# A third recursive product in a two-level Strassen-Winograd kernel, with differences written over the raw weights

## Chip, cores and metric

The kernel runs on one core of a Trainium2 chip. The metric is the device time of one execution in microseconds. TensorE (PE in the profile) multiplies, ScalarE (ACT) and VectorE (DVE) move results out of PSUM, the accumulators' memory of 8 banks, and form sums; SyncE (SP) issues the DMAs. Each engine takes its instructions in order; semaphores order the engines among each other.

## What is computed

```python
def _A_ref(x, wqkv, wo):
    q, k, v = ...x @ wqkv...           # 32 heads of 32
    phi = lambda t: jnp.where(t > 0, t + 1, jnp.exp(t)) + 1e-6
    pq, pk = phi(q), phi(k)
    kv = jnp.einsum("bhsd,bhse->bhde", pk, v)
    z = jnp.einsum("bhsd->bhd", pk)
    num = jnp.einsum("bhqd,bhde->bhqe", pq, kv)
    den = jnp.einsum("bhqd,bhd->bhq", pq, z)[..., None] + 1e-6
    return (num / den)... @ wo

def _B_ref(x, w_gate, w_up, w_down):
    return (_silu(x @ w_gate) * (x @ w_up)) @ w_down

xn = _layernorm(x)                     # x: 2048 x 1024
return x + _A_ref(xn, ...) * _silu(_B_ref(xn, ...))
```

The gate and up weights are 1024 x 3584, the down weights 3584 x 1024; inputs and output are bf16.

## The kernel before

**Stages.** Layer norm and the k and v projections with the sum over positions come first (some 120 us). Then a loop over weight blocks of 512 columns, `for k, n in order` (line 1431), for each of two halves of the positions, p = 0 and 1: gate blocks ("g", n), up blocks ("u", n), n = 0 to 6, and two blocks ("q", n) of the query projection. After ("u", 3) four attention-output pairs (`s_pair`, line 1221, one for each 512 positions) multiply the normalised queries by a matrix that holds kv and wo together. The gated products go to memory, and four groups (`Group`) read them back for the down projection.

**A pair.** Nearly every product of matrices is a 2 x 2 block product done with seven block products in place of eight. The seven products are called m = 1 to 7. Products 1, 2 and 4 use raw blocks of the stationary operand (here the weights), 5, 6, 7 and 3 use sums or differences of them, which `sums` (line 958) forms on VectorE. A `Set` (line 487) holds seven products for 128 stationary columns; its `step(m)` issues four matmuls 128x128 times 128x512 and the additions behind them. Two sets, 0 and 1, make a `Pair`: the step "7_1" is product 7 of set 1.

**A joint.** Products 1 and 5 of both sets of a pair are themselves one 2 x 2 block product, and `Joint` (line 551) does it with seven inner products of two matmuls of 256 columns each. Its four steps a to d need results of one another: step a issues inner products 1 and 5 and lets ScalarE copy both out of the bank, steps b and c each let VectorE add two results, step d is the last. "j1b" is step b of the joint for product 1. `inner_stat` (line 995) makes the sums of the stationary operand for the joints, `inner_move` (line 1022) those of the moving one (the activations), once for each half. After a joint for product 1 `put1` copies the result to a second bank; after one for product 5 `put5` copies it to SBUF.

**Order.** Within a pair the order is written out by hand: `LINK` (line 607) interleaves the end of one pair with the joints of the next, so that other matmuls stand between the steps of a joint ("n" marks steps of the next pair):

```python
LINK = "7_0 nj1a 3_0 7_1 nj1b nj5a 3_1 nj1c nj5b 4_0 nj1d nj5c 4_1 n2_0 nj5d n6_0 n2_1 n6_1".split()
```

On this a planner works when the program is built (`Plan.schedule`, line 91): it knows a cost of each instruction and fixes the order on each engine for good. PE may take an instruction early only within `WINDOW` = 6 groups of matmuls; VectorE and ScalarE take what is ready, most urgent first; a DMA is issued when what it overwrites is done with and its due time is near. `emit` (line 186) turns dependencies into semaphore waits.

**Weights.** `wload` (line 968) loads a block (1 MB) into one of two raw slots (`raw_ring`, 8 KB per partition) and writes four sums into one of two slots of `cmb_ring` (8 KB), and the joints' sums into `in_ring` (four slots of 2 KB, four sums each). Dependencies are tracked by region: a raw slot counts as one.

**Around the loop.** `m_build` (line 946) makes the combined matrix in 16 pieces that stand at steps of the first pairs (`BUILD`, line 1407). `recip` (line 1095) computes the denominators at ("g", 2), `normalise_part` (line 1125) multiplies the queries by them from ("u", 2) to ("g", 3). `phi_evac` (line 743) is the query's activation; with `split` ScalarE does a second pass over the tile in place of VectorE.

Of the kernel before, what the change touches and what calls it, by code (L numbers as in the profile page):

```python
# [239 lines left out]
def build_kernel(nc, A_x, A_wqkv, A_wo, B_w_gate, B_w_up, B_w_down, out, WINDOW=6, NWARM=14, NPE=4, LEAD=12.0):  # L240
# [12 lines left out]
    with ExitStack() as es:  # L253
# [178 lines left out]
        d_ring = Ring(TM, 4 * KB, 2 * KB, 2)  # L432
# [5 lines left out]
        x_ring = Ring(W, 36 * KB, 2 * KB, 4)  # L438
        xn_ring = Ring(W, 0, 2 * KB, 2)
        xs_ring = Ring(W, 44 * KB, 4 * KB, 2)  # L440
# [46 lines left out]
        class Set:  # L487
# [4 lines left out]
            def __init__(self, ops, evac, dring):  # L492
                self.ops, self.evac, self.dring, self.direct = ops, evac, dring, None
# [19 lines left out]

            def put5(self, e):
                self.s5 = s5_ring.take()
                act([bank_r[e]], [self.s5.r], self.s5.ap(F32), ps[e][:, :], ACT.Identity)
                bfree(e)

            def step(self, m):
# [11 lines left out]
                elif m == 6:  # L531
                    self.grp(6, self.b, False)
                    self.c = balloc()
                    tt([bank_r[self.b], self.s5.r], [bank_r[self.c]], ps[self.c][:, :], ps[self.b][:, :],
                       self.s5.ap(F32), ALU.add)
                elif m == 7:
                    self.grp(7, self.b, False)
                    if self.direct is not None:
                        self.direct(1, 1, self.b, self.s5)
                        return  # L540
                    d = self.dring.take()
                    tt([bank_r[self.b], self.s5.r], [d.r], d.ap(F32), ps[self.b][:, :], self.s5.ap(F32), ALU.add)
# [46 lines left out]
        class Pair:  # L589
# [3 lines left out]
            def __init__(self, s0, s1, joint, at):  # L593
                self.sets, self.joint, self.at = (s0, s1), joint, at

            def do(self, w):
                if w[0] == "j":
                    self.joint[w[1]].step("abcd".index(w[2]))
                else:
# [7 lines left out]
        LINK = "7_0 nj1a 3_0 7_1 nj1b nj5a 3_1 nj1c nj5b 4_0 nj1d nj5c 4_1 n2_0 nj5d n6_0 n2_1 n6_1".split()  # L607
        last_pair = [None]

        def feed(pair):  # L610

            prev = last_pair[0]
            if pair is None or not pair.joint:
                if prev is not None:
                    for w in TAIL:
                        prev.do(w)
# [3 lines left out]
            else:  # L620
                for w in LINK:
                    if w[0] == "n":
                        pair.do(w[1:])
                    elif prev is not None:
# [197 lines left out]
        def kv_set(u, w, stat):  # L822
# [16 lines left out]
            st = Set(ops, evac, d_ring)  # L839
# [118 lines left out]
        def sums(A, o, rd, wr):  # L958

            tt(rd, [wr[0]], o[0], A[0, 1], A[1, 1], ALU.add, True)  # L960
            tt(rd + [wr[0]], [wr[1]], o[1], o[0], A[0, 0], ALU.subtract, True)
            tt(rd, [wr[2]], o[2], A[0, 0], A[0, 1], ALU.subtract, True)
            tt(rd + [wr[1]], [wr[3]], o[3], A[1, 0], o[1], ALU.subtract, True)
# [4 lines left out]
        def wload(src, joint):  # L968
# [6 lines left out]
            cv = c.ap(FP16).rearrange("p (m w kt n) -> p m w kt n", m=4, w=2, n=128)  # L975
            cr = [c.sub(q * 2 * KB, 2 * KB).r for q in range(4)]
            sums({(k, i): v[:, :, 4 * k:4 * k + 4, i * 128:i * 128 + 128] for k in range(2) for i in range(2)},
                 [cv[:, q] for q in range(4)], [s.r], cr)

            def whole(m):  # L980
                if m in RAW_OF:
                    k, i = RAW_OF[m]
                    return v[:, :, 4 * k:4 * k + 4, i * 128:i * 128 + 128], s.r
                return cv[:, SUM_OF[m]], cr[SUM_OF[m]]

            def block(m):
                bl, r = whole(m)
                return (lambda k0, n, i: bl[:, i, k0:k0 + n, :]), r

            def stat(w, m):  # L990
                bl, r = whole(m)
                return [bl[:, w, q, :] for q in range(4)], r
            return stat, inner_stat(block, joint, 4, in_ring.take)

        def inner_stat(block, joint, kt, take):

            inner = {}
            for m in joint:
                bl, r = block(m)
                t = take()  # L1000
                n = kt // 2 * 256
                tv = t.ap(FP16, 0, 4 * n).rearrange("p (m kt n) -> p m kt n", m=4, n=128)
                tr = [t.sub(q * n, n).r for q in range(4)]
                A = {(k, i): bl(k * (kt // 2), kt // 2, i) for k in range(2) for i in range(2)}
                sums(A, [tv[:, q] for q in range(4)], [r], tr)
                inner[m] = (A, r, tv, tr)

            def jstat(m, k):
                A, r, tv, tr = inner[m]
                if k in RAW_OF:  # L1010
                    return [A[RAW_OF[k]][:, q, :] for q in range(kt // 2)], r
                return [tv[:, SUM_OF[k], q, :] for q in range(kt // 2)], tr[SUM_OF[k]]
            return jstat

        def xset(stat, w, xv, evac, dring):
# [4 lines left out]
            return Set(ops, evac, dring)  # L1020

        def inner_move(v, kt, at, raw=False, ms=(1, 5)):
# [17 lines left out]
        def in_places(arena, base, n):  # L1040
            return tuple(tuple((arena, base + (3 * m + q) * n) for q in range(3)) for m in range(2))
# [3 lines left out]
        def joint_of(jstat, xin, n, s0, s1):  # L1045
            def ops(m):
                def f(k):
# [4 lines left out]
            return {"1": Joint(ops(1), lambda w, b: (s0, s1)[w].put1(b)),  # L1052
                    "5": Joint(ops(5), lambda w, b: (s0, s1)[w].put5(b))}
# [17 lines left out]
        def q_load(s):  # L1071
            return wload(wqkv_v[:, :, s * 512:(s + 1) * 512], (1, 5))
# [10 lines left out]
        def q_pair(p, s, stats, at):  # L1083
            stat, jstat = stats

            def evac(w):
                def f(i, j, ap, r, bank):
                    g = 2 * (2 * s + w) + i
                    o, orr = pq_tile(p, g, j)
                    phi_evac(ap, r, o, orr, "ps" if bank is not None else "sb", i == 0)  # L1090
                return f
            s0, s1 = (xset(stat, w, XV[p], evac(w), d_ring) for w in range(2))
# [50 lines left out]
        def gu_load(k, n):  # L1143
            return wload((wg_v if k == "g" else wu_v)[:, :, n * 512:(n + 1) * 512], (1, 5))
# [13 lines left out]
        def gu_pair(p, kind, n, stats, at):  # L1158
# [38 lines left out]
            s0, s1 = (xset(stat, w, XV[p], (ev_g if kind == "g" else ev_u)(w), d_ring) for w in range(2))  # L1197
# [5 lines left out]
        def blocks(get, kt):  # L1203

            def block(m):
                ap, r = get(m)
                return (lambda k0, n, i: ap[:, k0:k0 + n, 128 * i:128 * i + 128]), r

            def stat(w, m):
                ap, r = get(m)  # L1210
                return [ap[:, q, 128 * w:128 * w + 128] for q in range(kt)], r
            return block, stat

        so_ring = Places([(TM, o * KB) for o in (8, 9, 12, 13)] + [(H, o * KB) for o in range(32, 40)], 1 * KB)
# [6 lines left out]
        def s_pair(g):  # L1221
            p, j0 = g // 2, g % 2
            A = {}
            for k in range(2):
                o = pq_off(p, k, j0)
                for i in range(2):
                    A[k, i] = (H.at(o, 4 * KB, FP16).rearrange("p (q t) -> p q t", t=512)[:, :, 256 * i:256 * i + 256],
                               H.reg(o, 4 * KB))
            c = ss_ring.take()
            cv = c.ap(FP16).rearrange("p (m q t) -> p m q t", m=4, t=256)  # L1230
            cr = [c.sub(q * 2 * KB, 2 * KB).r for q in range(4)]
            sums({q: a for q, (a, _) in A.items()}, [cv[:, q] for q in range(4)], [A[0, 0][1], A[1, 0][1]], cr)

            def get(m):
                return A[RAW_OF[m]] if m in RAW_OF else (cv[:, SUM_OF[m]], cr[SUM_OF[m]])
# [10 lines left out]
            s0, s1 = (xset(stat, w, MV, evac(w), d_ring) for w in range(2))  # L1246
            return Pair(s0, s1, joint_of(inner_stat(block, (1, 5), 4, in_ring.take), MIN, 2, s0, s1), {})
# [37 lines left out]
        DAT = (tuple((W, q * 3584) for q in range(3)), ((W, 28 * KB), (W, 28 * KB + 3584), (W, 43 * KB)))  # L1285
# [13 lines left out]
        hslots = Slots([(X, 0), (X, 7 * KB), (X, 14 * KB), (X, 21 * KB), (W, 20 * KB), (W, 36 * KB),  # L1299
                        (H, 7 * KB), (H, 14 * KB), (H, 21 * KB)], 7 * KB)  # L1300
        g_ring = Places([(W, o * KB) for o in (47, 48, 49, 50)], 1 * KB)
        sl_ring = Places([(W, o * KB) for o in (51, 27, 35, 19)], 1 * KB)
# [5 lines left out]
        class Group:  # L1308
# [50 lines left out]
            def dset(self, w):  # L1359
# [23 lines left out]
                return Set(ops, evac, d_ring)  # L1383
# [5 lines left out]
        XIN[1] = inner_move(XV[1], 4, in_places(W, 6 * KB, KB))  # L1389
# [4 lines left out]
        def fetch():  # L1394
            if lq:
                k, n = lq.popleft()
                return q_load(n) if k == "q" else gu_load(k, n)
# [5 lines left out]
        def build_m():  # L1403
            if mb:
                m_build(*mb.popleft())

        BUILD = {"2_0": [build_m], "6_0": [build_m], "2_1": [build_m] * 2, "6_1": [build_m] * 2}
        mb = deque((g, c) for c in range(2) for g in range(NG))
        AT = {("g", 0, 0): {"5_1": [kv_done], "3_0": [kvt]},
              ("g", 0, 1): BUILD, ("u", 0, 0): BUILD, ("u", 0, 1): BUILD,  # L1410
              ("g", 2, 0): {"6_1": [partial(recip, 0)]},
              ("g", 2, 1): {"6_1": [partial(recip, 1)]}}
        norm = [partial(normalise_part, p, j, half) for p in range(2) for j in range(2) for half in range(2)]
        for a, key in enumerate((("u", 2, 0), ("u", 2, 1), ("g", 3, 0), ("g", 3, 1))):
# [169 lines left out]
```

## Time and profile before

| | us |
|---|---|
| median of three runs (lowest, highest) | 717.33 (717.17, 718.4) |
| the profiled execution | 716.87 |
| its span, first to last instruction | 715.1 |
| TensorE busy | 705.0 |
| VectorE busy | 528.0 |
| ScalarE busy | 407.4 |

The profile is of one execution. A row of instructions has its start, its length, the engine, the source line (most lines are helpers': 229 issues matmuls, 359 ScalarE activations, 369 VectorE tensor-tensor operations, 372 DMAs), the operation, the tensors it writes and reads, its shape and how many alike were merged. X and P hold the activations of half 0 and 1, W the weights and their sums, H and TM other tiles, ps the PSUM banks. Rows overlap: an engine starts an instruction before the one ahead of it has ended.

### The profile page before, as it was taken

The page shows a single profiled execution, that of the slowest core. Times are in us where ns is not written, and L with a number is a line of the kernel's source. Part 1 is how long each engine was busy: PE and PEld are TensorE (multiplying, and loading weights), DVE is VectorE, ACT ScalarE, POOL GpSimd, SP SyncE. Part 2 cuts the span into 40 slices and gives each one's busy share as a digit, 9 for nine tenths or more (in the row PEclk, how much of TensorE's full clock was granted, in tenths as well). Part 3 has the DMA queues.
Part 4 walks back from the last instruction along what each step waited for, and adds up shares of the span by engine and source line. Part 5 has one row for each costly group of instructions (what it writes and reads, how often), then busy time and mean ns, then how long its engine had stood idle before and what let it go on. Part 6 is the DMA issues. An engine that isn't in the chain of part 4 may idle for free.

```text
span 715.1 us, 10861 instructions
## 1 busy us (share of the span) xinstructions
PE 705.0 (99%) x4035; PEld 385.8 (54%) x4064; DVE 528.0 (74%) x1181; ACT 407.4 (57%) x785; POOL 13.7 (2%) x35
## 2 busy tenths in 40 slices
PE   8999999999999999999999999999999999999997
PEld 3444445555555555555555555555554465565643
DVE  6998998676976797678998455957659994737442
ACT  4776655877876786679966665565662122121211
POOL 2111000000000000000000000000000000000000
PEclk9999999999999999999999999999999999999999
DMA  9443213113211330274225227554336646444412
GB/s 304 108 88 90 59 60 118 60 60 109 78 50 60 118 95 29 79 212 127 89 87 179 95 83 243 184 177 168 112 123 209 250 139 206 140 136 165 136 65 83
DMA packets 86869, 88.93 MB, mean 124 GB/s; under 512 B 17440, under 2 KB 82720, under 8 KB 86816
## 3 DMA queue, kind: packets, MB, share of 16 engines
q1 hardware_dynamic: 86816, 88.23, 39.0%
q8 instruction: 32, 0.52, 0.3%
q14 instruction: 21, 0.17, 0.1%
HBM read 61.87 MB, written 23.20 MB: 119 GB/s over the span
## 4 chain that ended last, share of the span: by engine, by line
PE 97%; DMA 1%; DVE 0%; SPq 0%; issue 0%; ACT 0%
PE ps L229 97%; DMA W<-in_A_x_dram 1%; SPq L372 0%; PE ps L236 0%; DVE stats L667 0%; DVE H L755 0%; ACT W L359 0%; DVE stats L671 0%; ACT ps L359 0%; DVE W L369 0%; DVE TM L369 0%; DVE mv L672 0%; DVE TM L754 0%; DVE veps L673 0%; DVE nmean L684 0%
## 5 line engine op out<-in xcount | busy, mean ns | idle before, releaser
L229 PE MATMUL ps<-P,W 128*128 128x512 f16 (+1 forms) x952 | 215.4, 350 | 0.0
L229 PE MATMUL ps<-X,W 128*128 128x512 f16 (+1 forms) x896 | 202.9, 351 | 0.0
L369 DVE TENSOR_TENSOR ps<-ps,TM 128x256 f32<-128x256 f32 (+1 forms) x246 | 130.5, 532 | 90.3 <-PE ps L229 64.2
L359 ACT ACTIVATE H<-ps 128x512 f16<-128x512 f32 (+2 forms) x225 | 133.5, 602 | 84.2 <-PE ps L229 83.7
L359 ACT ACTIVATE TM<-ps 128x512 f32<-128x512 f32 (+2 forms) x244 | 125.2, 531 | 33.3 <-PE ps L229 29.5
L229 PEld LDWEIGHTS ps<-P,W 128*128 128x128 f16 (+1 forms) x952 | 93.0, 98 | 73.8 <-ACT ps L359 0.3
L229 PEld LDWEIGHTS ps<-X,W 128*128 128x128 f16 (+1 forms) x896 | 87.4, 98 | 68.5 <-issue 0.2
L359 ACT ACTIVATE ps<-ps 128x512 f32<-128x512 f32 (+1 forms) x170 | 84.4, 496 | 62.2 <-PE ps L229 59.3
L369 DVE TENSOR_TENSOR W<-W 128x256 f16<-128x256 bf16 (+4 forms) x230 | 87.5, 418 | 25.9 <-ACT W L359 25.3
L369 DVE TENSOR_TENSOR H<-H 128x1024 f16<-128x1024 f16 (+3 forms) x143 | 85.7, 622 | 12.8 <-ACT H L359 8.1
L229 PE MATMUL ps<-H,X 128*128 128x512 bf16 (+3 forms) x376 | 80.0, 355 | 2.9 <-DVE nmean L684 0.9
L229 PE MATMUL ps<-W 128*128 128x256 f16 x444 | 78.5, 273 | 0.2
L229 PE MATMUL ps<-H,W 128*128 128x512 f16 (+3 forms) x365 | 76.8, 345 | 0.3
L229 PE MATMUL ps<-H 128*128 128x129 bf16 (+4 forms) x407 | 73.4, 315 | 0.4
L229 PEld LDWEIGHTS ps<-W 128*128 128x128 f16 (+1 forms) x444 | 43.2, 98 | 29.7 <-ACT TM L359 0.9
L229 PEld LDWEIGHTS ps<-H,X 128*128 128x128 f16 x388 | 37.3, 98 | 37.5 <-DVE H L755 1.2
L369 DVE TENSOR_TENSOR TM<-ps,TM 128x512 f32<-128x512 f32 x59 | 40.6, 688 | 21.0 <-PE ps L229 20.9
L229 PEld LDWEIGHTS ps<-H 128*128 128x128 f16 (+1 forms) x418 | 37.0, 98 | 31.8
L229 PEld LDWEIGHTS ps<-H,W 128*128 128x128 f16 x370 | 35.9, 98 | 32.0
L359 ACT ACTIVATE W<-ps 128x512 f16<-128x512 f32 x24 | 14.3, 597 | 54.5 <-PE ps L229 54.5
L369 DVE TENSOR_TENSOR H<-ps,TM 128x512 f16<-128x512 f32 (+1 forms) x35 | 24.1, 688 | 12.5 <-PE ps L229 12.1
L229 PE MATMUL ps<-W,H 128*128 128x512 f16 (+1 forms) x139 | 32.5, 368 | 0.0
(87 smaller groups left out, 461.1 us busy)
## 6 DMA issues: line engine op xcount, KB each, us to landing
h_scratch<-H SPq DMA_DIRECT2D x56, 256.0 KB, 2.2
W<-in_B_w_gate_dram SPq DMA_DIRECT2D x7, 1024.0 KB, 5.3
W<-in_B_w_up_dram SPq DMA_DIRECT2D x7, 1024.0 KB, 5.3
H<-in_B_w_down_dram SPq DMA_DIRECT2D x4, 1792.0 KB, 7.1
H<-h_scratch SPq DMA_DIRECT2D x7, 896.0 KB, 4.8
W<-in_A_x_dram SPq DMA_DIRECT2D x16, 256.0 KB, 3.2
H<-in_A_wqkv_dram SPq DMA_DIRECT2D x8, 512.0 KB, 8.1
H<-r_scratch SPq DMA_DIRECT2D x32, 128.0 KB, 3.2
```

The source lines that it names most:

```text
L229: last = h.matmul(o, l, r, start=st, stop=sp, skip_group_check=True)
L359: op = PL.op("act", reads, writes, lambda h: h.activation(o, i, func, **kw), nel(o) / 1200.0 + (0.055 if src == "ps" else 0.095))
L369: return dve(reads, writes, lambda h: h.tensor_tensor(o, a, b, op), nel(o), 1.92 if fast else 0.96)
```

## The change

The diff does these things:

- **A third joint.** `inner_stat` and `inner_move` also make the sums for product 2, and `joint_of` adds `Joint` "2". The result of joint 1 goes to SBUF (`keep1`) and stays in its bank; `put2` adds the two (for up blocks straight into the output tile, by `direct`). This holds for gate and up pairs of half 0 from ("g", 4) on, of half 1 from ("g", 2) on, and for all four attention-output pairs (`THIRD`, `S_THIRD`). Earlier pairs keep two joints.
- **In place.** In `wload` the difference for product 7 overwrites the raw block (0, 1), and in `inner_stat` the inner one overwrites a quarter of its block, so that `cmb_ring` slots have 6 KB and `in_ring` slots 1.5 KB. Regions are tracked in pieces of 256 bytes (`grains`). The sums for joints 5 and 2 of the next block are made from steps "j1d" and "j5d" on (`late`, `hook`).
- **Order.** New `LINK`, `LINK2` (three joints on both sides) and `LINK1`; `WINDOW` is 10. ("q", 1) stands ahead of ("g", 1); pieces of `m_build`, `recip` and `normalise_part` stand at other, earlier steps; `split` is chosen tile by tile.
- **Places.** Most rings move in SBUF; product 7 reuses the tile of product 5 in place of a `d_ring`.

```diff
-def build_kernel(..., WINDOW=6, NWARM=14, NPE=4, LEAD=12.0):
+def build_kernel(..., WINDOW=10, NWARM=14, NPE=4, LEAD=12.0):
...
+            def keep1(self, a):
+                self.b = a
+                self.s1 = s1_ring.take()
+                act([bank_r[a]], [self.s1.r], self.s1.ap(F32), ps[a][:, :], ACT.Identity)
+
+            def put2(self, b):
+                if self.direct is not None:
+                    self.direct(0, 0, b, self.s1)
+                    bfree(b)
+                    return
+                d = self.s1
+                tt([bank_r[b], d.r], [d.r], d.ap(F32), ps[b][:, :], d.ap(F32), ALU.add)
+                bfree(b)
+                self.evac(0, 0, d.ap(F32), d.r, None)
...
-        LINK = "7_0 nj1a 3_0 7_1 nj1b nj5a 3_1 nj1c nj5b 4_0 nj1d nj5c 4_1 n2_0 nj5d n6_0 n2_1 n6_1".split()
+        LINK = "nj1a 7_0 3_0 nj1b 3_1 nj5a nj5b 7_1 nj1c 4_0 4_1 nj5c nj1d nj5d n6_0 n2_0 n2_1 n6_1".split()
+        LINK2 = ("nj1a nj5a 7_0 nj1b 4_0 3_1 j2d nj5b nj1c nj2a 7_1 nj2b nj5c n6_0 nj2c nj1d nj5d 4_1 n6_1 n3_0"
+                 ).split()
+        LINK1 = "7_0 nj1a 3_0 7_1 nj1b nj5a 3_1 nj1c nj5b 4_0 nj1d nj5c 4_1 nj5d n6_0 nj2a nj2b n6_1 nj2c nj2d".split()
...
-        raw_ring = Places([(W, o * KB) for o in (12, 20)], 8 * KB)
-        cmb_ring = Places([(W, o * KB) for o in (28, 36)], 8 * KB)
-        in_ring = Places([(W, o * KB) for o in (44, 46, 48, 50)], 2 * KB)
+        raw_ring = Places([(W, o * KB) for o in (18, 44)], 8 * KB)
+        cmb_ring = Places([(W, o * KB) for o in (26, 38)], 6 * KB)
+        in_ring = Places([(W, 32 * KB + o * 1536) for o in range(4)], 1536)
...
             c = cmb_ring.take()
-            cv = c.ap(FP16).rearrange("p (m w kt n) -> p m w kt n", m=4, w=2, n=128)
...
+            cv = c.ap(FP16).rearrange("p (m w kt n) -> p m w kt n", m=3, w=2, n=128)
+            A = {(k, i): v[:, :, 4 * k:4 * k + 4, i * 128:i * 128 + 128] for k in range(2) for i in range(2)}
+            o = [cv[:, 0], cv[:, 1], A[0, 1].bitcast(FP16), cv[:, 2]]
...
+                if inplace:
+                    d = A[0, 1]
+                    o.insert(2, d.bitcast(FP16) if d.dtype != FP16 else d)
+                    wr.insert(2, R[0, 1])
+                sums(A, R, o, wr)
...
+        THIRD = (("g", 4), ("g", 2))
+        S_THIRD = True
+        S_AT = 3
...
-            return {"1": Joint(ops(1), lambda w, b: (s0, s1)[w].put1(b)),
-                    "5": Joint(ops(5), lambda w, b: (s0, s1)[w].put5(b))}
+            js = {"5": Joint(ops(5), lambda w, b: (s0, s1)[w].put5(b))}
+            if 2 in xin:
+                js["1"] = Joint(ops(1), lambda w, b: (s0, s1)[w].keep1(b))
+                js["2"] = Joint(ops(2), lambda w, b: (s0, s1)[w].put2(b))
+            else:
+                js["1"] = Joint(ops(1), lambda w, b: (s0, s1)[w].put1(b))
+            return js
...
-        order = [("g", 0), ("u", 0), ("q", 0), ("g", 1), ("u", 1), ("q", 1)] + [
-            (k, n) for n in range(2, NPAIR // 2) for k in "gu"]
+        order = [("g", 0), ("u", 0), ("q", 0), ("q", 1), ("g", 1), ("u", 1), ("g", 2), ("u", 2), ("g", 3), ("u", 3), ("g", 4), ("u", 4), ("g", 5), ("u", 5), ("g", 6), ("u", 6)]
...
+        J_FREE, J_FREE1 = {5: "j1d", 2: "j5d"}, {5: "j1d"}
...
+                if (k, n) == THIRD[p]:
+                    XIN[p].update(inner_move(XV[p], 4, in_places(W, 9 * p * KB, KB)[2:], ms=(2,)))
```

More of the change, by code (lines that the diff above doesn't have):

```diff
@@ L620, in feed @@
             else:
-                for w in LINK:
+                third = [x is not None and "2" in (x.joint or ()) for x in (prev, pair)]
+                link = LINK if not third[1] else LINK2 if third[0] else LINK1
+                early = REST[:6] if third == [True, False] else [w[1:] for w in LINK2] if third[0] else ()
+                for w in REST:
+                    if w in early and w not in prev.did:
+                        prev.do(w)
+                for w in link:
                     if w[0] == "n":
                         pair.do(w[1:])
-                    elif prev is not None:
+                    elif prev is not None and w not in prev.did and (w[0] != "j" or "2" in prev.joint):
                         prev.do(w)
@@ L990, in stat, with inner_stat, make @@
             def stat(w, m):
[L991 to L995, printed above, removed]
+                return [bl[m][:, w, q, :] for q in range(4)], rg[m]((w,), 0, 4)
+            return stat, inner_stat(block, joint, 4, in_ring.take, True, late)
+        def inner_stat(block, joint, kt, take, inplace=False, late=()):
             inner = {}
-            for m in joint:
[L999 to L1006, printed above, removed]
+            h = kt // 2
+            def make(m):
+                t = slots[m]
+                n = h * 256
+                ns = 3 if inplace else 4
+                tv = t.ap(FP16, 0, ns * n).rearrange("p (m kt n) -> p m kt n", m=ns, n=128)
+                o = [tv[:, q] for q in range(ns)]
+                wr = [t.sub(q * n, n).r for q in range(ns)]
+                A, R = {}, {}
+                for k in range(2):
+                    for i in range(2):
+                        A[k, i], R[k, i] = block(m)(k * h, h, i)
+                if inplace:
[3 more added lines that the diff above has]
+                sums(A, R, o, wr)
+                inner[m] = (A, R, o, wr)
+            slots = {m: take() for m in joint}
+            for m in joint:
+                if m not in late:
+                    make(m)
@@ L1016, in ops, with hook, xset @@
+            jstat.late = {m: partial(make, m) for m in late}
+            return jstat
+        def hook(at, late, steps):
+            at = {w: list(fs) for w, fs in at.items()}
+            for m, w in steps.items():
+                if m in late:
+                    at.setdefault(w, []).append(late[m])
+            return at
+        def xset(stat, w, xv, evac):
             def ops(m):
```

200 lines of the change are left out of this document (119 added, 81 removed).

## The prediction

> **What bounds the kernel now.** I read the page first, then the chain of waits, then what TensorE waited for.
>
> ```profile
> span 715.1 us, 10861 instructions
> PE 705.0 (99%) x4035; PEld 385.8 (54%) x4064; DVE 528.0 (74%) x1181; ACT 407.4 (57%) x785; POOL 13.7 (2%) x35
> ...
> PEclk9999999999999999999999999999999999999999
> ...
> PE 97%; DMA 1%; DVE 0%; SPq 0%; issue 0%; ACT 0%
> ```
>
> TensorE (PE) is busy 99% of the span at the full granted clock, and the chain that ends last is 97% PE. Busy time alone does not show that PE is never kept waiting; the next rows do, one piece of the chain in order of time and the complete list of PE's waits.
>
> ```profile
> 160.04 385.16 PE ps L229 x2281
> ...
> PE ps L229 <- POOL ident L412: 1.4, 1, 1.4
> PE ps L229 <- DVE nmean L684: 0.9, 1, 0.9
> PE ps L229 <- DMA H<-in_A_wqkv_dram: 0.7, 1, 0.7
> PE ps L229 <- ACT X L359: 0.5, 1, 0.5
> PE ps L229 <- ACT ps L359: 0.2, 1, 0.2
> ```
>
> From 160 to 545 us PE runs 2281 matmuls without one wait; the waits add up to 3.7 us and belong to the start. So a matmul removed is worth its whole interval, and a new wait costs its whole length. The changed pairs lie in this piece. The interval of a matmul is start to start, not the length of a row (in a stream the ends overlap):
>
> ```profile
> 402.61 0.60 PE L229 MATMUL ps<-X,W 128*128 128x256 f16 x4
> 403.04 0.38 PE L229 MATMUL ps<-W 128*128 128x256 f16 x2
> 403.26 0.38 PE L229 MATMUL ps<-X,W 128*128 128x256 f16 x2
> 403.48 1.03 PE L229 MATMUL ps<-H 128*128 128x512 f16 x4
> 404.34 0.38 PE L229 MATMUL ps<-W 128*128 128x256 f16 x2
> ```
>
> Four wide matmuls (512 columns) take 404.34 - 403.48 = 0.86, so 0.215 each; eight narrow ones (256) take 403.48 - 402.61 = 0.87, so 0.109 each.
>
> **The change on TensorE.** Outer product 2 of a pair now is eight wide matmuls (two sets, four each). As a third `Joint` it is seven products of two narrow ones, 14 in all: 8 x 0.215 = 1.72 against 14 x 0.109 = 1.53. That saves 0.20 us a pair. It is done for p = 0 from ("g", 4) on (6 pairs), for p = 1 from ("g", 2) on (10), and for the 4 attention-output pairs: 20 pairs, 160 wide matmuls out, 280 narrow in, 160 x 0.2155 - 280 x 0.109 = 34.5 - 30.5 = 3.9 us.
>
> The Trainium skill has a rule against this trade: "TensorE: Matmul & The Clock Gate", section Back-to-back issue gap, gives 131 ns a matmul at 512 columns and 81 ns at 128 as sustained spacing in streams that load weights each time. Read on a straight line that is an estimate of 98 ns at 256, and a pair would lose 14 x 98 - 8 x 131 = 0.32 us, 6.4 us in all. This trace disagrees with the rule: its rows have 215 and 109 ns, each matmul with its own weight load.
>
> **The change on VectorE.** Each new joint adds two 256-column additions (steps b and c), and `put2` adds product 1, kept in SBUF, to product 2: two 512-column additions. For twenty joints that is 40 of each. The sums for the new product add 56 of 128x256 in half precision and 14 of 128x512; two phi instructions go. The in-place differences replace as many that wrote elsewhere. Intervals, again start to start:
>
> ```profile
> 481.99 0.69 DVE L369 TENSOR_TENSOR ps<-ps,TM 128x512 f32<-128x512 f32 x1
> 482.59 0.68 DVE L369 TENSOR_TENSOR H<-ps,TM 128x512 f16<-128x512 f32 x1
> ...
> 485.29 0.43 DVE L369 TENSOR_TENSOR ps<-ps,TM 128x256 f32<-128x256 f32 x1
> 485.63 0.68 DVE L369 TENSOR_TENSOR H<-H 128x1024 f16<-128x1024 f16 x1
> ...
> 487.87 1.09 DVE L369 TENSOR_TENSOR W<-W 128x256 f16<-128x256 f16 x5
> 488.88 0.68 DVE L369 TENSOR_TENSOR H<-H 128x1024 f16<-128x1024 f16 x1
> ...
> 492.18 1.28 DVE L369 TENSOR_TENSOR W<-W 128x1024 f16<-128x1024 bf16 x2
> 493.38 0.69 DVE L369 TENSOR_TENSOR ps<-ps,TM 128x512 f32<-128x512 f32 x1
> L369 DVE TENSOR_TENSOR W<-W 128x512 f16<-128x512 f16 x32 | 13.5, 421 | 25.6 <-ACT W L359 25.3
> L369 DVE TENSOR_TENSOR P<-H 128x1536 f16<-128x1536 bf16 x2 | 1.9, 955 | 0.2 <-PE ps L229 0.2
> ```
>
> So 0.60 (512, f32), 0.34 (256, f32), 1.01/5 = 0.20 (256, f16), 0.60 (1024, f16). A row's length exceeds the interval by 0.09 (0.69 against 0.60), so the last two rows give 0.34 and 0.87. Added: 40 x 0.60 + 40 x 0.34 + 56 x 0.20 + 14 x 0.34 - 2 x 0.6 = 52 us, nearly all in the piece without waits. There VectorE has room, unevenly:
>
> ```profile
> 260.00:541.00 281.00, 281.00 (x1687) 159.71 (x1686) 207.54 (x463) 195.78 (x404) 0.00 (x0) 1.00 0.42 136
> ...
> 340.00:360.00 20.00, 20.00 (x118) 11.20 (x117) 19.84 (x51) 19.34 (x39) 0.00 (x0) 1.00 0.26 84
> 360.00:380.00 20.00, 20.00 (x118) 11.31 (x117) 20.00 (x48) 12.73 (x26) 0.00 (x0) 1.00 0.35 113
> ```
>
> (Columns: PE, weight loads, VectorE, ScalarE, POOL busy, clock, DMA share, GB/s.) Of 281 us VectorE is idle 73; (207.5 + 52)/277 = 94% is left busy at most. At 340 to 380 it is already full, and PE did not wait. A full VectorE costs nothing, then, as long as no matmul needs one of its queued results too early. PE's queue is in order too: behind a matmul that waits stand all later ones, and ScalarE and VectorE run dry behind them, so a wait is paid once and in full. It can be counted: between a matmul that releases a VectorE instruction and a later one that waits for a later instruction of that in-order queue, all VectorE work between must fit into the matmul work between. In the changed order two stretches do not fit.
>
> First, from the end of product 6 (second set) of ("u", 3), p = 0, to product 4 (first set) of the third attention-output pair stand 125 VectorE instructions: 25 x 0.605 + 24 x 0.60 + 43 x 0.20 + 24 x 0.34 + 9 x 0.34 = 49.4. The ends add 0.35: a matmul's tail beyond its interval (1.03 - 0.86 = 0.17), the last row's 0.09, and hand-overs of about 0.1. Matmul work there is 49.6. PE is 0.2 short; I take 0.3.
>
> Second, around ("g", 5): from the third joint's step c of ("u", 4) to that of ("g", 5), p = 1, 53 instructions, 12 x 0.605 + 12 x 0.34 + 14 x 0.20 + 13 x 0.60 + 2 x 0.87 = 23.7, with the ends 24.1, against 23.4 of matmuls: 0.7 short. Six of them prepare the down weights (`wd_sum`). Inside this stretch a matmul of joint 5 step b stands right behind the last of its step a, whose ScalarE copy it needs:
>
> ```profile
> L359 ACT ACTIVATE TM<-ps 128x256 f32<-128x256 f32 x76 | 28.9, 380 | 0.0
> L359 ACT ACTIVATE ps<-ps 128x256 f32<-128x256 f32 x76 | 28.5, 374 | 27.4 <-PE ps L229 27.3
> ```
>
> That is a matmul's tail 0.17 + 0.37 + about 0.1 = 0.6 of waiting, most of it time that the 0.7 counts already; if nothing of it is shared, the two make 1.3. The same count over the order of before finds no place after 160 us that doesn't fit, as the trace says.
>
> So waits of 0.3 + 0.7 = 1.0 at least, 1.6 with the unshared one; 0.4 more for chains through two queues, which this count cannot see, is a choice. I take 1.4, toward the upper end.
>
> **Edits that cost nothing.** ScalarE gets 40 narrow copies (15 us) and loses two table loads; `keep1` writes SBUF where `put1` wrote PSUM, 598 against 595 ns by rows of the same shape. It is 57% busy. Its cover, were it gone, is priced by the 0.6 above. The two reciprocal steps and the normalisation move one to two stages earlier, and ("q", 1) comes before ("g", 1); their 8 + 32 small transfers pass SP ahead of other weight loads, at most 40 x 0.4 us of issue spread over 100 us; the price if one load is late is the rival below. The planner's window grows from 6 to 10: during the start the same matmuls stand in another order; I take 0, between -0.9 and +0.9, the longest wait on VectorE among PE's waits above. The last ScalarE and two VectorE instructions, and the last store, are the same.
>
> **Sum.** -3.9 + 1.4 = -2.5 us. The profiled execution took 716.87 us, 1.77 of it outside its span, and lies 0.46 below the median of 717.33; span 712.6, so 714.4 for that execution and 714.8 against the median.
>
> **Rivals.**
> 1. All waits vanish (hand-overs shorter than I allow, slack elsewhere): 717.33 - 3.9 = 713.4. For it: full VectorE at 360 to 380 without a wait. Against: two counted stretches that are too long.
> 2. VectorE's queue loses time whenever it must itself wait. At the start it was less than full while PE did wait:
>
> ```profile
> 20.00:60.00 40.00, 39.59 (x216) 19.35 (x219) 38.21 (x99) 28.11 (x42) 5.88 (x8) 1.00 0.41 87
> ```
>
> 38.21 of 40 is 95.5%. At that share the two stretches of 49.4 and 23.7 stretch by 2.3 and 1.1 beyond the 1.0 already counted, giving -3.9 + 1.0 + 3.4 = +0.5, about 717.8: within 0.2%. Against: 19.84 and 20.00 of 20 above.
> 3. On the other side, weight sums that come late. Differences now overwrite raw weights, so the slot stays taken until the last product that uses it, and the matmul work from there to the first one that needs the next block's inner sums falls from 16.2 us to 13.7 for the loads of ("g", 5) to ("u", 6). In it must fit the load and seven sums (3 x 0.60 + 4 x 0.20 = 2.6).
>
> ```profile
> DMA to landing us min/median/max: 5.0/5.3/8.1
> ...
> 440.00:460.00 20.00, 20.00 (x117) 11.12 (x115) 18.30 (x38) 11.95 (x25) 0.00 (x0) 1.00 0.66 216
> ```
>
> With the median landing 13.7 - 5.3 - 2.6 = 5.8 us are over for other work queued ahead on VectorE; with the longest, 3.0. It decides once more than that stands ahead; VectorE at 94% can hold that much. A block late by 1 to 2 us in each of these four costs 4 to 8: 717.33 - 2.5 + 4 to 8 = 718.8 to 722.8. Against: with 2.5 us more of margin PE never waited for a weight block after the start.
> 4. Narrow matmuls lose their rate where three joints interleave. At 1.72/14 = 0.123 each the saving is gone; with a weight load of 0.098 (93.0 us of 952 loads) exposed on each of the 120 added, 717.33 - 3.9 + 11.8 = 725.
>
> ```profile
> L229 PEld LDWEIGHTS ps<-P,W 128*128 128x128 f16 (+1 forms) x952 | 93.0, 98 | 73.8 <-ACT ps L359 0.3
> ```
>
> Against: 0.109 held in rows where narrow products of two joints alternate. The skill's spacing above would end here too; by the trace I give it 2%.
>
> **Chances.** Forecast (waits of 0.6 to 2.4 us, so 714.0 to 715.9): 0.55. Rival 1: 0.14. Rival 2 or other waits that eat the saving: 0.15. Rival 3: 0.12. Rival 4: 0.02. The change not doing what it says: 0.02, since the instruction order shows the 280 narrow matmuls. A measurement of this kernel can tell about 0.2% (1.4 us) from no change: faster below 715.9 is 0.55 + 0.14 = 0.69, within 0.16 (0.15 and half of the last 0.02), slower 0.15. The range 713.3 to 718.0 leaves out rivals 3 and 4 and a little on the fast side; the forecast's own range is 714.0 to 715.9.
>
> **What would show it.** Matmul rows: 160 wide fewer, 280 narrow more, intervals still 0.215 and 0.109, or rival 4. VectorE's busy time up by some 50 us, full from about 340 to 400 us. PE's waits: new ones of 0.3 and 0.6 us, on VectorE in the attention-output stretch and on ScalarE or VectorE in the neighbourhood of 458 us, none on a weight load. Waits on sums of weights past 440 us would mean rival 3; many small waits on VectorE spread from 330 to 540, rival 2. The prediction is wrong if waits after 160 us exceed 2.4 us.

## The result, and the profile after

| kernel | median us | lowest to highest | runs | ratio to before (95% interval) |
|---|---|---|---|---|
| before | 717.71 | 717.17 to 718.4 | 6 | |
| after | 714.40 | 714.02 to 714.64 | 6 | 0.9954 (0.9942 to 0.9967) |

The changed kernel is 3.3 us faster, and the whole interval lies below 1. The forecast was 714.8 (714.0 to 715.9). The profiled execution of after took 714.41 us.

First the page of after: span, and the busy time of each engine with its instructions.

```profile
span 712.7 us, 11321 instructions
...
PE 703.1 (99%) x4184; PEld 397.1 (56%) x4184; DVE 573.6 (80%) x1329; ACT 413.6 (58%) x809; POOL 12.8 (2%) x35
```

VectorE has 148 instructions and 45.6 us more (528.0 before), ScalarE 24 and 6.2 us more, and the span is 2.4 us shorter: TensorE still sets the time, and most of the added work is under it. There are 120 more weight loads (PEld, 4064 before), as 280 narrow matmuls in and 160 wide ones out should give.

Next, the start of matmuls in the long piece of after, in the same view as the prediction's rows (start, length, what):

```profile
457.45 0.81 PE L229 MATMUL ps<-X,W 128*128 128x512 f16 x3
458.10 0.82 PE L229 MATMUL ps<-P,W 128*128 128x256 f16 x6
459.38 0.39 PE L229 MATMUL ps<-P,W 128*128 128x256 f16 x2 [0.46 <-ACT ps L359]
459.66 0.39 PE L229 MATMUL ps<-W 128*128 128x256 f16 x2
```

Three wide matmuls take 458.10 - 457.45 = 0.65, 0.216 each, as before. Six narrow ones at 0.109 should be followed by the next at 458.10 + 0.65 = 458.75; it starts at 459.38. So 0.63 us is lost here. The bracket shows only 0.46, since it counts from the end of the row, with the tail of the last matmul in it. This is how each wait below is measured: start to start, less the number of matmuls times their interval.

Then PE's waits, the complete list (engine, line, what it waited for; total, times, longest):

```profile
PE ps L229 <- POOL ident L412: 1.4, 1, 1.4
PE ps L229 <- DMA H<-in_A_wqkv_dram: 1.2, 1, 1.2
PE ps L229 <- DVE H L786: 0.7, 1, 0.7
PE ps L229 <- ACT X L359: 0.5, 1, 0.5
PE ps L229 <- ACT ps L359: 0.5, 1, 0.5
PE ps L236 <- DVE veps L704: 0.3, 1, 0.3
PE ps L229 <- DVE ps L369: 0.2, 1, 0.2
```

All but one belong to the first 40 us; the new one is `ACT ps`, the wait at 459 just read. No weight block is in the list after the start. A second new wait is too short for it, and the chain of after shows where it is:

```profile
127.97 211.48 PE ps L229 x1300
...
354.66 0.61 DVE H L369
355.27 0.05 issue
355.32 103.61 PE ps L229 x666
458.93 0.02 issue
458.96 0.38 ACT ps L359
459.33 0.05 issue
459.38 248.53 PE ps L229 x1438
```

At 355.32 the chain passes from a VectorE instruction to PE, which means that this matmul was held by VectorE. The narrow pair ahead of it starts at 354.88, and 354.88 + 2 x 0.109 = 355.10: it waits 0.22 us. After that PE runs to 459, and then to the last eviction at 708, with nothing else on the chain. The chain before 355 leaves PE at 339.45 and goes through VectorE from 341.16 on, for 14 us, though PE lost nothing there: a chain follows the last releaser, and a full queue then looks like the limit. Its length is no price; the 0.22 is.

Last, the windows of after (columns as in the prediction: PE, weight loads, VectorE, ScalarE, POOL busy, clock, DMA share, GB/s), beside which the prediction shows those of before:

```profile
340.00:360.00 20.00, 19.94 (x126) 12.07 (x125) 20.00 (x49) 13.11 (x29) 0.00 (x0) 1.00 0.25 80
360.00:380.00 20.00, 20.00 (x129) 12.43 (x127) 20.00 (x53) 14.70 (x32) 0.00 (x0) 1.00 0.26 86
380.00:400.00 20.00, 20.00 (x131) 12.62 (x130) 20.00 (x55) 14.79 (x32) 0.00 (x0) 1.00 0.53 171
440.00:460.00 20.00, 19.54 (x128) 12.07 (x126) 19.71 (x44) 11.30 (x25) 0.00 (x0) 1.00 0.59 197
```

For 60 us VectorE is busy in every moment, and PE does not slow down: from 360 to 400 it is busy throughout.

**A finer measure.** Spans differ by up to 2 us between executions of one kernel, as the experiments will show, and this hides what one wait costs. The difference lies at the start, and a stretch that leaves it out repeats far better: from the first of eight transposes near 127 us to the last ScalarE eviction. The two rows that bound it, before and then after (the stretch is from start to start):

```profile
126.69 0.61 PE L236 MATMUL ps<-ident,H 128*128 128x128 f16 x8
...
710.29 0.60 ACT L359 ACTIVATE W<-ps 128x512 f16<-128x512 f32 x1 [2.42 <-PE ps L229]
```

```profile
127.36 0.61 PE L236 MATMUL ps<-ident,H 128*128 128x128 f16 x8
...
707.94 0.60 ACT L359 ACTIVATE W<-ps 128x512 f16<-128x512 f32 x1 [0.91 <-PE ps L229]
```

583.60 before, 580.58 after: 3.02 us less, each from its one profiled execution. Matmul work explains -3.94, so 0.92 must have come back as waiting; read one by one, the waits at 355 (0.22) and at 459 (0.63 and 0.05) make 0.90.

### The profile page after: what moved, and what is told of

Same layout as the page of the kernel before. It is cut to its first block, busy times and chain, and to the rows that moved or that the text cites. A ratio compares the mean times of both kernels' runs of the same rounds, so it can differ in the third digit from the quotient of the medians.

```text
span 712.7 us, 11321 instructions
## 1 busy us (share of the span) xinstructions
PE 703.1 (99%) x4184; PEld 397.1 (56%) x4184; DVE 573.6 (80%) x1329; ACT 413.6 (58%) x809; POOL 12.8 (2%) x35
## 4 chain that ended last, share of the span: by engine, by line
PE 93%; DVE 4%; DMA 1%; ACT 1%; SPq 0%; issue 0%
PE ps L229 93%; DVE H L369 2%; DMA W<-in_A_x_dram 1%; DVE ps L369 1%; DVE W L369 1%; SPq L372 0%; DVE H L786 0%; PE ps L236 0%; DVE stats L702 0%; DVE stats L698 0%; ACT H L359 0%; ACT X L359 0%; DVE TM L369 0%; ACT W L359 0%; DVE TM L785 0%
## 5 line engine op out<-in xcount | busy, mean ns | idle before, releaser
L359 ACT ACTIVATE TM<-ps 128x512 f32<-128x512 f32 (+2 forms) x293 | 147.4, 529 | 44.5 <-PE ps L229 42.7
L359 ACT ACTIVATE H<-ps 128x512 f16<-128x512 f32 (+2 forms) x192 | 112.5, 602 | 50.9 <-PE ps L229 48.9
L369 DVE TENSOR_TENSOR W<-W 128x256 f16<-128x256 f16 (+5 forms) x270 | 97.8, 395 | 23.5 <-ACT W L359 19.8
L359 ACT ACTIVATE ps<-ps 128x256 f32<-128x256 f32 (+1 forms) x150 | 67.5, 451 | 70.7 <-PE ps L229 69.0
L369 DVE TENSOR_TENSOR H<-H 128x1024 f16<-128x1024 f16 (+5 forms) x152 | 86.6, 589 | 8.8 <-ACT H L359 7.0
L229 PE MATMUL ps<-W 128*128 128x256 f16 x525 | 91.7, 273 | 0.0
L229 PE MATMUL ps<-H,W 128*128 128x512 f16 (+3 forms) x420 | 90.8, 351 | 0.2 <-DVE ps L369 0.2
L369 DVE TENSOR_TENSOR TM<-ps,TM 128x512 f32<-128x512 f32 x83 | 56.7, 685 | 22.8 <-PE ps L229 22.3
L229 PEld LDWEIGHTS ps<-W 128*128 128x128 bf16 (+1 forms) x525 | 51.0, 98 | 29.6 <-DVE ps L369 1.7
L359 ACT ACTIVATE H<-TM 128x512 f16<-128x512 f32 x58 | 36.4, 629 | 11.3 <-DVE TM L369 11.2
```

Source lines behind the costliest of these rows:

```text
L229: last = h.matmul(o, l, r, start=st, stop=sp, skip_group_check=True)
L359: op = PL.op("act", reads, writes, lambda h: h.activation(o, i, func, **kw), nel(o) / 1200.0 + (0.055 if src == "ps" else 0.095))
L369: return dve(reads, writes, lambda h: h.tensor_tensor(o, a, b, op), nel(o), 1.92 if fast else 0.96)
```

## Experiments

The theory: the gain is the narrow matmuls' shorter total and nothing else, and it is kept only where VectorE's queue between two matmuls fits into the matmul work between them. The rivals: the gain comes from the new order, the window or the in-place sums; or VectorE, now full, costs time wherever it stands. All edits below are to the kernel after unless another is named. "Stretch" is the measure above. e1 to e4 ran on one chip and e5 to e8 on another, each time with before beside them (medians 717.66 and 717.54); after was not run again there.

| kernel | median us | ratio to before (95% interval) | stretch us | against after |
|---|---|---|---|---|
| before | | | 583.60 | +3.02 |
| after | 714.40 | 0.9954 (0.9942 to 0.9967) | 580.58 | |
| e1: third joints in the last up block alone | 718.00 | 1.0003 (0.9994 to 1.0012) | 584.16 | +3.58 |
| e2: down sum later | 714.45 | 0.9951 (0.9939 to 0.9964) | 579.89 | -0.69 |
| e3: more VectorE work, attention | 720.89 | 1.0044 (1.0032 to 1.0057) | 586.94 | +6.36 |
| e4: more VectorE work, down | 714.26 | 0.9950 (0.9937 to 0.9962) | 580.58 | 0.00 |
| e5: window 6 | 717.59 | 1.0001 (0.9992 to 1.0010) | 584.15 | +3.57 |
| e6: e2 and third joints from ("g", 1) | 713.42 | 0.9949 (0.9937 to 0.9962) | 579.88 | -0.70 |
| e7: attention pairs with two joints | 715.50 | 0.9973 (0.9962 to 0.9984) | 581.49 | +0.91 |
| e8: e6 and half 0 from ("g", 2) | 716.10 | 0.9981 (0.9972 to 0.9990) | 582.22 | +1.64 |

**e1: all of the change but eighteen of the third joints.** Window, in-place sums, places and the order of two-joint pairs stay; product 2 is an outer product again in eighteen of the twenty pairs. The two pairs of ("u", 6) keep their third joint, and `LINK2`, the order between two pairs with three joints, is left in one place.

```diff
-        THIRD = (("g", 4), ("g", 2))
-        S_THIRD = True
+        THIRD = (("u", 6), ("u", 6))
+        S_THIRD = False
```

> The changed kernel with the third joint in the last up block alone (2 pairs in place of 20); the new order, the window of 10 and the in-place differences stay. Theory (the gain is the narrow matmuls' shorter total): 18 x 8 wide more and 18 x 14 narrow fewer, 18 x 0.197 = 3.5 us more matmul work, less the 0.9 us of waits that the three-joint pairs have in the changed kernel, plus up to 0.9 for places that the same count finds too short here (around 460 us and 530 us): 714.4 + 2.6 to 3.5 = 717.0 to 717.9, as slow as before. Rival (the gain comes from the new order, the window and the finer regions): it stays near 714.4, at most 715.

Measured: 718.0, no different from before, and 0.1 above the range that was expected; the rival's 715 is out. The stretch is 584.16, which is 0.56 above that of before: the two pairs that keep their joint take off 0.39, short waits at 243, 460 and 532 us (0.18, 0.41, 0.29) put 0.88 on, and less than 0.1 is left over. So the window, the in-place sums and the new order of two-joint pairs bring nothing by themselves, and there is no gain without the narrow matmuls.

**e2: the down weights' sum later.** Six VectorE instructions of `wd_sum` leave the stretch that was counted 0.7 us too long.

```diff
             if (k, n) == ("g", S_AT + 1):
                 for nm, u in (("R01", 0.0), ("R00", -15.0), ("R11", -30.0), ("R10", -45.0)):
                     wd_load(nm, u)
+            if (k, n) == ("u", 6):
                 wd_sum("T1", "R01", "R00")
```

> The changed kernel with the first sums of the down weights (6 VectorE instructions) made after the last up block and not after (g, 4). Theory (the wait of 0.62 us at 459 us comes from VectorE's queue being 53 instructions and 0.7 us too long there, and these 6 are among them): the wait goes and TensorE's order there changes so that no joint's step b stands right behind its step a; 714.4 - 0.6 = 713.8. The wait of 0.23 us in the attention-output stretch stays. Rival (it is the hand-written order of the three joints that leaves too little between steps a and b): the wait stays near 459 us or comes back at the other p = 1 pairs, 714.4 or more.

Measured: stretch -0.69. The window of e2 around the place, and the complete list of its waits:

```profile
440.00:460.00 20.00, 20.00 (x131) 12.57 (x129) 19.64 (x46) 11.32 (x25) 0.00 (x0) 1.00 0.58 192
```

```profile
PE ps L229 <- DMA H<-in_A_wqkv_dram: 1.9, 1, 1.9
PE ps L229 <- POOL ident L412: 1.4, 1, 1.4
PE ps L236 <- DVE veps L704: 1.0, 1, 1.0
PE ps L229 <- ACT X L359: 0.5, 1, 0.5
PE ps L229 <- DVE ps L369: 0.2, 1, 0.2
```

PE is busy for 20.00 of 20 where it was 19.54, and `ACT ps` is gone. PE's rows at the same place show how:

```profile
459.50 0.60 PE L229 MATMUL ps<-P,W 128*128 128x256 f16 x4
459.93 1.03 PE L229 MATMUL ps<-X,W 128*128 128x512 f16 x4
460.80 0.38 PE L229 MATMUL ps<-P,W 128*128 128x256 f16 x2
```

Four wide matmuls (0.87 us) now stand between step a of that joint and its step b, and cover the ScalarE copy; in after, step b (459.38) follows step a at once. So ScalarE is rightly named as what PE waited for, but what made the wait was VectorE work of another stage: it is all that the edit moves, and without it the planner's order has other matmuls to put there. That VectorE itself would have held PE for the counted 0.7 is not shown. The two waits that the prediction counted there (0.7 and 0.6) were one. The stretch moves as expected (0.6); the median does not, 714.45 where 713.8 was expected. In the profiled run the start took back what was gained: 1.9 us of waiting for the first `wqkv` block and 1.0 for `veps`, where after had 1.2 and 0.3. That the unprofiled runs lost it in the same way wasn't seen.

**e3: twice the attention stages' sums.** The outer sums of an attention-output pair are made twice with the same operands, 16 VectorE instructions more, 9.6 us by their intervals, in the first of the two stretches.

```diff
-            sums(A, {q: r(0, 4, (0, 1)) for q, r in R.items()}, [cv[:, q] for q in range(4)],
-                 [r(0, 4, (0, 1)) for r in cr])
+            for _ in range(2):
+              sums(A, {q: r(0, 4, (0, 1)) for q, r in R.items()}, [cv[:, q] for q in range(4)],
+                 [r(0, 4, (0, 1)) for r in cr])
```

> The changed kernel with the four outer sums of each attention-output pair made twice: 16 VectorE instructions of 0.60 us, 9.6 us, in a stretch of some 55 us where VectorE is full. Theory (VectorE there has no room left): most of it lands on TensorE, +5 to +9 us, 719 to 723, in many waits of 0.2 to 0.7 us on VectorE between 345 and 400 us. Rival (VectorE's busy share overstates its load, as 340 to 380 us before was full without a wait): under +2 us.

Measured: stretch +6.36 us, twice the gain of 3.02, as expected. Its windows, and PE's waits on VectorE after the start:

```profile
360.00:380.00 20.00, 18.15 (x113) 10.04 (x111) 20.00 (x50) 11.83 (x25) 0.00 (x0) 1.00 0.18 59
380.00:400.00 20.00, 19.08 (x117) 10.15 (x115) 20.00 (x50) 13.23 (x28) 0.00 (x0) 1.00 0.57 186
```

```profile
PE ps L229 <- DVE ps L369: 1.7, 5, 0.5
...
PE ps L229 <- DVE TM L369: 1.0, 4, 0.4
PE ps L229 <- DVE H L369: 0.6, 1, 0.6
```

The list makes 3.3 us, because its waits count from the ends of rows and the shortest are left out; start to start, PE loses 6.2 us at seventeen places between 355 and 404, where after loses 0.22. VectorE reads 20.00 as it does in after, but its matmul records in these 40 us are 230, where after has 260. The busy time of a full engine does not say how far it lags; the matmuls that get through beside it do.

**e4: more VectorE work where it has room.** A sum of the down stage is made three times in three of four groups: 24 instructions more, 12.8 us.

```diff
                 self.mk(self.s[5], self.s[0, 1], self.s[1, 1], ALU.add)
+                for _ in range(2 if self.g else 0):
+                    self.mk(self.s[5], self.s[0, 1], self.s[1, 1], ALU.add)
```

> The changed kernel with one sum of each of the last three groups of the down projection made three times: 24 VectorE instructions, 18 of 0.60 and 6 of 0.34 us, 12.8 us, where VectorE is idle for most of the time. Theory (VectorE's work costs nothing where its queue has room): 714.4 within 0.4. Rival (VectorE's work costs time wherever it is put, by memory or by delaying results): +1 us or more.

Measured: stretch 580.58, equal to after to 0.01 us. More VectorE work than e3 added costs nothing here, so the price of VectorE work is set by the stretch that it stands in and not by its amount.

**e5: the window.** Third joints as in after, but the planner looks 6 ahead.

```diff
-def build_kernel(..., WINDOW=10, NWARM=14, NPE=4, LEAD=12.0):
+def build_kernel(..., WINDOW=6, NWARM=14, NPE=4, LEAD=12.0):
```

> The changed kernel with the planner's window of 6 in place of 10, all matmuls the same. Measured from the eight transposes before the first up block to the last ScalarE activation, since the start varies by 2 us from run to run; the changed kernel has 580.58 us there, before 583.60. Theory (the new joints need other matmuls between their steps, and the window of 10 lets the planner put them there): waits of 0.65 on ScalarE copies at four p = 1 pairs from (g, 2) to (u, 3), some 1.5 in the attention-output stretch and 0.9 around 459, in place of 0.85 in all; +3 to +4.5 us, 583.6 to 585.1, as slow as before or slower: the narrow matmuls alone would gain nothing. Rival (the window only shuffles matmuls that are ready anyway): 580.6 within 0.5.

Measured: 717.59, no gain left. The list of waits and one of its places:

```profile
PE ps L229 <- ACT ps L359: 2.8, 6, 0.7
```

```profile
280.97 1.46 PE L229 MATMUL ps<-P,W 128*128 128x256 f16 x8
282.89 0.39 PE L229 MATMUL ps<-P,W 128*128 128x256 f16 x2 [0.46 <-ACT ps L359]
283.19 0.39 PE L229 MATMUL ps<-W 128*128 128x256 f16 x2
```

In four pairs of half 1 (at 282, 306, 330 and 354 us) a step of a joint stands right behind the step whose ScalarE copy it needs. The first row holds four narrow and four wide matmuls (a row shows the shape of its first): 4 x 0.109 + 4 x 0.216 = 1.30, so the next should start at 280.97 + 1.30 = 282.27, and it starts 0.62 later. That is the 0.6 which the prediction priced for that copy without cover. The row at 283.19 is 0.08 late as well; in the four places the two gaps make about 0.68 each. Longer or shorter waits at 215, 357 and 462 us (0.19, 0.46, 0.9) were there too; the one at 357 had been expected larger. All together make 4.3 of the 4.5 us that the stretch lacks (584.15 - 583.60 + 3.94). In this order the third joint and the wider window are of use only together: e1 has the window without eighteen of the joints, e5 the joints without the window, and each ends where before did. Whether an order written for a window of 6 would do as well was not tried.

**e6: two pairs more.** The edit of e2, and third joints for half 1 from ("g", 1) on.

```diff
-        THIRD = (("g", 4), ("g", 2))
+        THIRD = (("g", 4), ("g", 1))
```

> The changed kernel with the down-weight sums late, and product 2 by inner products for p = 1 from (g, 1) on and not (g, 2), two pairs more. Theory: 2 x 0.197 = 0.39 less matmul work, no new wait, since VectorE has room before (g, 2), and the wait at 459 us gone: 580.58 - 0.39 - 0.69 = 579.5 in the same stretch, 713.3 in all. Rival (VectorE's added sums at (g, 1) and (u, 1) delay the normalisation that now stands there): waits between 205 and 260 us, 580 or more.

Measured: stretch 579.88, the same as e2, where two pairs should have given another 0.39. This was a miss. The matmul rows of e6 around the new pairs, and ScalarE's there:

```profile
251.63 0.73 PE L229 MATMUL ps<-P,W 128*128 128x256 f16 x4
252.27 0.39 PE L229 MATMUL ps<-W 128*128 128x256 f16 x2
252.50 0.38 PE L229 MATMUL ps<-P,W 128*128 128x256 f16 x2
```

```profile
249.67 1.97 ACT L359 ACTIVATE H<-H,zc 128x512 bf16<-128x512 bf16 x3
251.51 0.41 ACT L359 ACTIVATE ps<-ps 128x256 f32<-128x256 f32 x1
```

Four narrow matmuls need 0.44, and the next starts after 0.64: 0.20 lost there, and 0.17 at 242.8 in the same way. Together they eat all but 0.02 of the 0.39. Both stand where the rival expected waits, but on another engine: the joint's ScalarE copy (251.51) comes late behind three ScalarE passes of the normalisation (249.67). Its median of 713.42 is the lowest measured, but its interval is that of e2 and of after; these three can't be told apart by runs.

**e7: the attention pairs with two joints.**

```diff
-        S_THIRD = True
+        S_THIRD = False
```

> The changed kernel with two joints in the four attention-output pairs, everything else as it is. Theory: 4 x 0.197 = 0.79 more matmul work and the wait of 0.23 us in that stretch gone; 0.2 to 0.4 may come at 405 us, where the next block's sums now stand, and the wait at 459 may be 0.2 longer: 580.58 + 0.6 to 1.1 = 581.2 to 581.7 in the stretch. Rival (VectorE is so full there that the third joint costs more than it saves): 580.4 or less.

Measured: stretch +0.91. Four pairs at 0.197 cost 0.79, the wait at 355 is gone (-0.22), and new ones of 0.25 at 412 and 0.1 at 460 came. The window of e7:

```profile
380.00:400.00 20.00, 20.00 (x118) 11.32 (x117) 13.11 (x32) 13.44 (x27) 0.00 (x0) 1.00 0.40 134
```

VectorE is busy 13.11 of 20 us, where after has 20.00, and this room is worth nothing here: the filled engine of after buys 0.8 us of matmuls for 0.22 of waiting.

**e8: four pairs more on top of e6.**

```diff
-        THIRD = (("g", 4), ("g", 1))
+        THIRD = (("g", 2), ("g", 1))
```

> As the run with one more block, and product 2 by inner products for p = 0 from (g, 2) on and not (g, 4), four pairs more: 6 x 0.197 = 1.18 less matmul work than the changed kernel. Theory (the saving ends where VectorE's queue is full): the count of VectorE work between two matmuls is 0.7 us too long at about 260 us and 3.4 too long from 322 to 385, where it was 0.3; 580.58 - 1.18 - 0.69 + 0.7 + 3.1 = 582.5, slower than the changed kernel in spite of less matmul work. Rival (count too pessimistic, TensorE is the bound): 578.7 to 579.5.

Measured: stretch 582.22, near the 582.5 expected and +1.64 against after, though its matmul work is 6 x 0.197 = 1.18 less. The window of e8, and two of the matmuls that waited:

```profile
360.00:380.00 20.00, 18.55 (x115) 10.65 (x114) 20.00 (x51) 11.68 (x24) 0.00 (x0) 1.00 0.21 72
```

```profile
362.65 1.04 PE L229 MATMUL ps<-P,W 128*128 128x512 f16 x4 [0.58 <-DVE H L369]
...
374.73 0.39 PE L229 MATMUL ps<-TM,H 128*128 128x256 f16 x2 [0.53 <-DVE H L369]
```

The added pairs of half 0 stand ahead of the attention stages, and what they put into VectorE's queue has not drained when those begin: six waits between 358 and 376 us make 2.9 us (3.4 counted), two more at 261 and 264 us 0.56 (0.7 counted). It is the first counted stretch again, lengthened from its front instead of from within as in e3. Where the change stops adding third joints is therefore near the point where they stop paying.

## Why the prediction was right

1. **What bounds the kernel.** TensorE in the piece without waits, so that a matmul is worth its interval. Shown by e1 and e7: eighteen pairs without their third joint are 3.58 us longer, four are 0.91, where 0.197 a pair makes 3.55 and 0.79. The waits that went and came make -0.90 and +0.88 in e1, -0.22 and +0.35 in e7, which leaves 0.05 and 0.01 unread.
2. **-3.9 us of matmul work.** The intervals stayed at 0.216 and 0.109. Rival 4 is out, and with it the estimate of +6.4 us from the Trainium skill, "TensorE: Matmul & The Clock Gate", section Back-to-back issue gap: the 131 ns that it gives at 512 columns is not the spacing of this stream, which is 216.
3. **52 us more on VectorE.** Each count was as predicted; the page says 45.6. The intervals count a row after the one before it, while busy time counts an overlap once: some seventy rows that stood alone and now overlap a neighbour by 0.09 would make up the 6, which is argued and not shown. Its full stretch came at 340 to 400 us, as said.
4. **Two stretches too long, waits of 1.4.** One wait came in each: 0.22 on VectorE at 355 (0.3 taken, 0.2 counted) and 0.68 on ScalarE at 459 (0.7 counted for VectorE). This term was mis-sized: 0.90 in place of 1.4. The allowance of 0.4 for chains through two queues, a choice, did not appear, and the 0.7 and the 0.6 were one wait. The counts fit in size better than in mechanism. The first runs on to the third attention-output pair, but its wait stands at the start of the first, two pairs (some 23 us of matmuls) earlier. And the second has the length of a ScalarE copy without cover, the prediction's 0.6: the same 0.62 and then 0.05 to 0.06 stand at the four places of e5, where no count names VectorE. That it came so near to the 0.7 is partly luck; what e2 shows is that those VectorE instructions bring it about.
5. **Edits at nothing.** Narrow copies, moved steps, `keep1`: no wait in the list but the one of point 4 comes from them. The window was priced at 0 between -0.9 and +0.9, for its effect on the start, and no run has it alone. In e1 it comes with the new order, and their waits of 0.88 lie behind the start, where the prediction had no price for the window; e5 shows that with third joints the window carries 3.6 us. The prediction read the new order with the window in it, so the sum held, but it did not say what the window was worth there. In-place sums of 128x1024 take 680 ns against 683: no cost.
6. **The sum.** -2.5 was forecast for the profiled execution, with a span of 712.6; 712.7 was found. That it came so close is luck: the stretch gave -3.0, the smaller waits of point 4, and this execution came to the transposes 0.67 us later than that of before did. The medians, in which such starts are averaged, lie 3.3 apart. The forecast's 714.8 also started from 717.33, the median of three runs; six runs of before have 717.71.
7. **The rivals.** Rival 1 (no waits) is out by the two that are there. Rival 2 (VectorE's queue loses time when it waits) is out for this kernel: 60 us at 20.00 of 20, and PE lost 0.22 there. Rival 3 (weight sums late) is out: no weight block and no sum of weights among PE's waits past 440 us. These are the waits of one profiled execution; that the rivals stay out under slower transfers was not tried.

## What to carry to other kernels

Where one engine runs without a wait, count for every pair of dependent matmuls what stands between them in the other engine's in-order queue, and compare it with the matmul work between. That count found the two stretches of this change and came near to what they lost, and near to e8's (3.4 and 0.7 counted, 2.9 and 0.56 lost), though not to the place and engine of each wait. Busy shares (a full VectorE that costs 0.22 in after, 6.4 us more in e3) told nothing. A wait named after one engine can be made by work on another that was put into the same stretch, here by way of the order that a planner then chose (e2), so try to move work out of the stretch before speeding up the engine that is named. A trade of TensorE time for VectorE work pays until the fullest stretch overflows, and then the added pairs lose more than they win (e8: 2.3 us longer than e6 for 0.8 us less of matmuls).

## What was not expected of the hardware

The start of an execution varies more than most effects studied here. The kernel after, e2 and e4 differ only in what comes long after the transposes near 127 us, and reached them at 127.36, 128.75 and 126.44. PE's wait for the first `wqkv` block follows it: 1.2, 1.9, and none in the list of e4. From there to the last eviction after and e4 both take 580.58, and to the matmul that is held at 355 after, e2 and e4 all take 227.96. So spans or medians of a few runs don't resolve much less than 1 us here, while a stretch between two fixed instructions resolves 0.1.
